# Start of a Strassen w_out stage: two operand sums formed earlier, operands halved ahead of weight tiles, two weight loads issued sooner

## The chip, the cores and the metric

The kernel runs on one core of one Trainium2 chip. TensorE (PE) multiplies, with its weight loads shown apart as PEld; VectorE (DVE), ScalarE (ACT) and GpSimd (POOL) work on tiles; SyncE (SP) issues all DMAs here. The metric is the device time of one execution in microseconds, lower is better.

## The reference

A block with attention in a sliding window, and a gated MLP beside it, over 2048 tokens of width 576, all in float32. What the change touches is the last product of the MLP and the end of the block.

```python
z1 = z[..., :Fh]                       # Fh = 2304
z2 = _layernorm(z[..., Fh:], axis=-1)
g = jnp.einsum("ts,bsf->btf", w_sp, z2) + b_sp[None, :, None]
return jnp.einsum("bsf,fd->bsd", z1 * g, w_out)     # the w_out stage
...
s = _A_ref(xn, A_wqkv, A_wo)
g = _silu(_B_ref(xn, B_w_in, B_w_sp, B_b_sp, B_w_out))
return x + s * g
```

## The kernel before, in words

Every float32 product is made as three matmuls in a reduced format: each operand is halved into an upper half (`act.activation` with a copy on ACT, line 115) and a lower half (source minus upper half on DVE, line 116). PE multiplies upper by upper, upper by lower and lower by upper. `split` (lines 114 to 116) is this pair, so every halved tile costs one ACT and one DVE instruction, in this order, and the third matmul of each block needs DVE's.

The stage before (`acc`, line 1429) is the token mixing with `w_sp`; its gated result y is stored to DRAM (`y_d<-z1t`, line 1365). The w_out stage then multiplies y (2304 by 2048) with w_out (2304 by 576), in 2 by 2 blocks. Tokens come in eight pairs p of two groups of 128 rows. Pair 0 is computed directly: four operands (a12, a11, a21, a22), each with two products of 27 matmuls, 54 per step. Pairs 1 to 7 use the Strassen-Winograd scheme: seven products P1 to P7 of 27 matmuls, whose left operands are blocks of y or sums of them, and whose right operands are blocks of w_out or the sums T1 to T4 prepared earlier in DRAM (`t_d`).

The list `SEQ` (line 1303) fixes the order of the steps: pair 0's four, then of pair 1 P4, P1, P6, P2, P5, P7, then of pair 2 P4, P1, then P3 of pair 1, P6 of pair 2, and so on. Step i is matmuled, and then the operand of step i+3 is formed by `formed(i + 3)`, which calls `y_form`. Operands live in three tiles o0, o1, o2 in turn, so o(i mod 3) is free when step i has been multiplied. The engines are not reordered by a scheduler here: each runs its instructions in the order in which the code is written, and so does SP with its DMAs.

Blocks of y for a pair are loaded (`y_load`, line 1317) into fixed places: a11 and a21 into the tile `zr`, a22 and a12 into the tile `u2` (named `u2_15512` in the orders, `u` in the trace); from pair 2 on one of a12 and a22 goes to a `wr` buffer instead. When `y_form` makes P1's operand, three sums follow on DVE, in place (lines 1327 to 1329): a22 becomes a21 + a22, a21 becomes a11 - a21, a11 becomes the new a22 - a11. The new a11 is P6's operand, the new a21 is P7's, the new a22 is P5's.

Weights come in 13 parts of up to five blocks of 128 rows: parts 7 to 12 are fetched by `w_fetch` (line 1272) into one of two `wr` buffers and halved by `w_halve` into b5 and w0 to w4. Parts 9 to 12 (w1 to w4) hold T2 and T1, which P6 and P5 use. The sum T3, for P7, goes in three pieces (`t3_fetch`, line 1288; `t3_halve`) over the place of B12, through the same two `wr` buffers: a fetch waits until the part that was in its buffer has been halved. w2, w3 and w4 lie in the pool `yp`, which takes over the memory of the pool `wk`, where the tiles `z1t` were; so w2 is written only when the last stores `y_d<-z1t` have read them.

Rows are finished by `finish` (lines 1498 to 1506): DVE multiplies the attention output `sv` by the gate `gs` (line 1501) and adds `xr`, the input (line 1502), SP stores the row (line 1503), and `load_end` loads `sv` and `xr` of the next row (lines 1491, 1492).

Of the kernel before, what the change touches and what calls it, by code (L numbers as in the profile page):

```python
# [12 lines left out]
ALU = mybir.AluOpType  # L13
# [51 lines left out]
def kernel(  # L65
# [14 lines left out]
    act, dve, pool, pe, sp = nc.scalar, nc.vector, nc.gpsimd, nc.tensor, nc.sync  # L80
# [155 lines left out]
    with ExitStack() as early:  # L236
# [281 lines left out]
        with ExitStack() as ph:  # L518
# [259 lines left out]
            def finish(u, ou):  # L778

                g, half = UNITS[u]  # L780
                cs = slice(half * HS, half * HS + HS)
                den = aa.tile([P, HS // 32], F32, name="den")
                rp = ap_.tile([P, HS], F32, name="rp", bufs=1) if u < NU - 1 else f32(slots[4][:, 0:HS])
                def invert():
                    dve.reciprocal(den, den)
                    t = use("dve", 270) - clock + 300
                    after(t + (1500 if u < NU - 2 else 300), lambda: sp.dma_start(r_d[u].rearrange("h (a b) -> (h a) b", b=HS // 32), den))
                    for i in range(4):
                        after(t + (FETCH_AT if u < NU - 2 else 4500) + 400 * i, partial(sums, i))

                def sums(i):
                    sp.dma_start(rp[32 * i:32 * i + 32, :], r_d[u][i:i + 1, :].to_broadcast([32, HS]))

                def divide(a, n=4):
                    hs = slice(a * HS // n, (a + 1) * HS // n)
                    pool.tensor_tensor(ou[:, hs], ou[:, hs], rp[:, hs], ALU.mult)
                    use("pool", 2900 / n)

                def store(i):
                    h = 4 * g + i  # L800
                    sp.dma_start(o_d[h * DH:(h + 1) * DH, cs], ou[32 * i:32 * i + DH, :])

                if u == NU - 1:
                    def put_last():
                        dve.reciprocal(den, den)
                        sp.dma_start(r_d[u].rearrange("h (a b) -> (h a) b", b=HS // 32), den)

                    last.extend([lambda: sp.dma_start(den, ou[DH::32, :]), put_last,
                                 lambda: [sums(i) for i in range(4)], lambda: [divide(a, 2) for a in range(2)],
                                 lambda: [store(i) for i in range(4)]])  # L810
                else:
                    after(busy["act"] - clock + 1000, lambda: sp.dma_start(den, ou[DH::32, :]))
                    sooner = 10000 if u == NU - 2 else 0
                    after(max(INVERT_AT - sooner, 4500), invert)
                    parts[u] = [partial(divide, a) for a in range(4)] + [partial(store, i) for i in range(4)]
                    for ns in DIVIDE_AT:
                        after(ns - sooner + (3500 if sooner else 0), partial(part, u))
# [388 lines left out]
    with ExitStack() as ph:  # L1206
# [58 lines left out]
        def w_fetch(i, home):  # L1265
            n = 3 if i == 12 else 5
            w_raws[i] = w_raw(home, i, n)
            done = 0
            while done < n:
                o, k0 = divmod(5 * i + done, 9)  # L1270
                m = min(n - done, 9 - k0)
                sp.dma_start(w_raws[i][:, done:done + m], w_rows(W_ORDER[o], k0, m))
                done += m

        def w_halve(i, home, name):
            raw = w_raws.pop(i)
            n = raw.shape[1]
            t = home.tile([P, 8 * ZW if home in (xp, zc) else n * D], F32R, name=name)[:, :n * D]
            t = t.rearrange("p (a k c) -> p a k c", a=2, c=288)
            split(t[:, 0], t[:, 1], raw)  # L1280
            w_tiles.append(t)
# [16 lines left out]
        quads, operands, homes = {}, {}, {}  # L1298
# [10 lines left out]
        def y_load(p, name):  # L1309
            i, j = int(name[1]) - 1, int(name[2]) - 1  # L1310
            t = p + 4 * (p // 4) + 4 * i
            if p > 1 and name == ("a12", "a22")[p % 2]:
                q = homes["o2"].tile([P, 1440], F32, name="wr", bufs=2)[:, :9 * P]
            else:
                q = QUAD_AT[name]
            quads[p, name] = q = q.rearrange("p (f t) -> p f t", t=P)
            sp.dma_start(q, y_d[j * FB:(j + 1) * FB, t * P:(t + 1) * P].rearrange("(f p) t -> p f t", p=P))

        def y_form(i):
            p, prod = SEQ[i]  # L1320
            home = yw if i % 3 < 2 else homes["o2"]
            o = home.tile([P, 2304], F32R, name=f"o{i % 3}", bufs=1).rearrange("p (a f t) -> p a f t", a=2, t=P)
            q = {name: quads.get((p, name)) for name in QUAD_AT}
            split(o[:, 0], o[:, 1], q[OF.get(prod, prod)])
            operands[p, prod] = o
            if prod == "P1":
                dve.tensor_tensor(q["a22"], q["a21"], q["a22"], ALU.add)
                dve.tensor_tensor(q["a21"], q["a11"], q["a21"], ALU.subtract)
                dve.tensor_tensor(q["a11"], q["a22"], q["a11"], ALU.subtract)
            if prod == "P2":  # L1330
                dve.tensor_tensor(q["a12"], q["a12"], q["a11"], ALU.subtract)
# [80 lines left out]
        def run_lazy(n):  # L1412
            for _ in range(n):
                if lazy:
                    lazy.pop(0)()
# [71 lines left out]
        def load_end():  # L1487
            if row_order:
                r = end_rows(*row_order.pop(0))
                t = [yp.tile([P, D], F32, name=n, bufs=1 + (n == "xr")) for n in ("sv", "xr", "gs")]  # L1490
                sp.dma_start(t[0], s_d[r, :])
                sp.dma_start(t[1], x[r, :])
                ends.append((r, *t))
# [4 lines left out]
        def finish(c0=0, c1=D):  # L1498
            r, sv, xr, gs = ends[0]
            cs = slice(c0, c1)  # L1500
            dve.tensor_tensor(sv[:, cs], sv[:, cs], gs[:, cs], ALU.mult)
            dve.tensor_tensor(xr[:, cs], xr[:, cs], sv[:, cs], ALU.add)
            sp.dma_start(out[r, cs], xr[:, cs])
            if c1 == D:
                ends.pop(0)
                load_end()

        def small_tile(p, name):
            small[p, name] = t = (right if name in ("t1", "t4") else yp).tile([P, 288], F32, name=name, bufs=1)
# [53 lines left out]
        for i, (p, prod) in enumerate(SEQ):  # L1563
            if p == 0:
                first_pair(i, prod)
                if i == 0:
                    y_load(1, "a11")
                    y_load(1, "a21")
                    w_halve(8, right, "w0")
                    w_fetch(9, right)  # L1570
                formed(i + 3)
                if i == 0:
                    run_lazy(6)
                    w_halve(9, right, "w1")
                    w_fetch(10, right)
                    run_lazy(len(lazy))
                    gates.close()
                    yp = open_pool(ph, "yp")
                    load_end()
                    y_load(1, "a12")  # L1580
                if i in (1, 3):
                    silu_of(0, banks[f"C{i // 2 + 1}1"][:, :288])
                    silu_of(1, banks[f"C{i // 2 + 1}2"][:, :288])
                if i == 1:
                    w_fetch(11, right)
                    w_halve(10, yp, "w2")
                    finish()
                if i == 2:
                    w_fetch(12, right)
                    w_halve(11, yp, "w3")  # L1590
                    t3_fetch(right, T3_PARTS[0])
                if i == 3:
                    finish()
                    w_halve(12, yp, "w4")
                    t3_fetch(right, T3_PARTS[1])
                continue
            o = operands.pop((p, prod))
            c = product(o, (p, BANK_OF[prod]), W_OF[prod])
            sums = sum_up(p, prod, c)
            if i == 5:  # L1600
                t3_halve(T3_PARTS[0])
                t3_fetch(right, T3_PARTS[2])
            if i in (6, 7):
                t3_halve(T3_PARTS[i - 5])
            formed(i + 3)
            for half in sums:
                silu_of(*half)
            if prod in ("P7", "P3"):
                if (p, prod) == (LAST, "P3"):
                    finish(288, D)  # L1610
                else:
                    finish()
            if (p, prod) == (LAST, "P2"):
                finish(0, 288)
# [71 lines left out]
```

## Time and profile before

| what | us |
|---|---|
| median of three runs | 1860.63 (1852.94 to 1866.33) |
| the profiled execution | 1859.84 |
| its span, first to last instruction | 1857.8 |
| what lies around the span | 2.0 |
| first matmul of the w_out stage (c, line 1520) | 1641.82 |
| start of the last run of matmuls without a wait | 1705.79 |

Times inside the trace count from the start of the span. A row of a timeline gives start, duration, engine, line, operation and tiles, and in brackets how long the engine sat idle before it and what ended that. Starts of consecutive matmuls lie closer together than their durations, since they are pipelined. SPq rows are the issue of a DMA, not its transfer.

### The profile page before, as it was taken

What the parts mean: (1) busy time and instruction counts of PE and PEld (TensorE: products, weight loads), DVE (VectorE), ACT (ScalarE), POOL (GpSimd) and SP (SyncE); (2) the same over time, 40 slices, a digit from 0 to 9 for tenths busy, and PEclk for the clock granted to TensorE, in tenths of its full rate; (3) what the DMA queues carried; (4) which work ended last, traced back from release to release, by engine and by line L of the source; (5) the groups of instructions that cost most, each with busy time, mean ns of one, the idle gap of its engine ahead of it and who ended that gap; (6) DMA issues with size and microseconds to landing.
All of it is one profiled execution on the core that took longest, in us unless ns stands there. A gap on an engine that the chain in (4) does not pass through costs nothing.

```text
span 1857.8 us, 38152 instructions
## 1 busy us (share of the span) xinstructions
PE 1819.5 (98%) x14357; PEld 1584.6 (85%) x14357; DVE 1138.2 (61%) x2283; ACT 946.8 (51%) x1756; POOL 433.3 (23%) x507
## 2 busy tenths in 40 slices
PE   8999999999999999999999999999999999998998
PEld 8999999997777777776988878888888888898998
DVE  6321333457766777761246788667876567758876
ACT  5433222315666576677467566465554544444443
POOL 3332333434465455555000000121200000000000
PEclk9999999999999999999999999999999999999999
DMA  8895688887576666655876777789776556796554
GB/s 272 190 234 161 232 283 281 297 251 218 155 190 168 189 180 184 182 156 145 254 247 227 238 238 245 257 290 304 252 260 234 186 182 199 251 264 186 161 159 133
DMA packets 266920, 405.75 MB, mean 218 GB/s; under 512 B 52336, under 2 KB 180592, under 8 KB 266608
## 3 DMA queue, kind: packets, MB, share of 16 engines
q1 hardware_dynamic: 266736, 403.32, 70.3%
q8 instruction: 113, 1.85, 0.4%
q14 instruction: 71, 0.58, 0.1%
HBM read 285.35 MB, written 117.09 MB: 217 GB/s over the span
## 4 chain that ended last, share of the span: by engine, by line
PE 81%; DMA 6%; DVE 6%; ACT 3%; SPq 2%; issue 2%; POOL 0%; ACTq 0%; DVEq 0%; POOLq 0%
PE acc L1429 35%; PE mb L206 9%; PE c L1520 7%; PE ma L206 7%; PE ma L669 6%; PE mb L669 5%; PE ops L750 4%; PE tps L722 2%; PE sp L598 2%; PE wops L1155 1%; SPq L363 1%; DMA st_d<-qkhl 1%; DMA z_d<-z1o 1%; DVE junk L602 1%; PE ma L380 1%
## 5 line engine op out<-in xcount | busy, mean ns | idle before, releaser
L1429 PE MATMUL acc<-sph,zh 128*128 128x512 f32 x1008 | 392.3, 389 | 1.7 <-ACT so L1188 1.7
L1429 PE MATMUL acc<-spl,zh 128*128 128x512 f32 x1008 | 392.7, 390 | 1.2 <-DVE spl L116 1.0
L1429 PE MATMUL acc<-sph,zl 128*128 128x512 f32 x1008 | 392.2, 389 | 0.0
L602 DVE CUSTOM_DVE_ANT_0 junk<-sp,band 128x384 bf16<-128x384 f32 (+1 forms) x512 | 276.3, 540 | 113.4 <-PE sp L598 32.6
L726 ACT ACTIVATE pt<-tps 128x384 f32<-128x384 f32 (+2 forms) x576 | 231.3, 441 | 119.4 <-PE tps L722 75.8
L116 DVE TENSOR_TENSOR spl<-spr,sph 128x1024 fp32r<-128x1024 f32 x168 | 209.9, 1249 | 41.9 <-ACT sph L115 40.9
L669 PE MATMUL mb<-b,z1wh 64*128 64x512 f32 x648 | 224.5, 399 | 2.1 <-ACT z1o L674 1.7
L1429 PEld LDWEIGHTS acc<-spl,zh 128*128 128x128 f32 x1008 | 189.2, 188 | 42.4 <-DVE spl L116 3.2
L669 PE MATMUL ma<-b,z1wh 64*128 64x512 f32 x648 | 223.9, 398 | 0.7 <-ACT zt L946 0.4
L1429 PEld LDWEIGHTS acc<-sph,zh 128*128 128x128 f32 x1008 | 189.2, 188 | 41.1 <-ACT so L1188 2.2
L1429 PEld LDWEIGHTS acc<-sph,zl 128*128 128x128 f32 x1008 | 189.2, 188 | 39.4
L115 ACT ACTIVATE zh<-b 128x384 fp32r<-128x384 f32 x168 | 87.4, 520 | 209.2 <-PE acc L1429 209.1
L115 ACT ACTIVATE sph<-spr 128x1024 fp32r<-128x1024 f32 x168 | 176.0, 1047 | 16.2 <-DMA spr<-in_w_sp_dram 8.5
L722 PE MATMUL tps<-att 56*128 56x384 f32 (+1 forms) x576 | 176.7, 345 | 3.2 <-DMA att<-mhl 1.6
L116 DVE TENSOR_TENSOR zl<-b,zh 128x384 fp32r<-128x384 f32 x168 | 99.6, 593 | 122.7 <-ACT zh L115 122.6
L598 PE MATMUL sp<-att 54*128 54x384 f32 (+1 forms) x512 | 160.7, 348 | 1.6 <-DVE mx L602 1.5
L1520 PE MATMUL c<-b,o 128*128 128x288 f32 x1056 | 143.8, 295 | 2.7 <-DVE o L116 1.8
L1520 PEld LDWEIGHTS c<-b,o 128*128 128x128 f32 x1056 | 140.9, 188 | 3.6 <-DVE o L116 2.3
L947 DVE BATCH_NORM_STATS2 st<-zt 128x6 f32<-128x384 f32 x96 | 49.3, 548 | 132.0 <-ACT zt L946 131.7
L669 PE MATMUL ma<-b,z1wl 64*128 64x512 f32 x324 | 128.0, 395 | 0.0
L669 PE MATMUL mb<-b,z1wl 64*128 64x512 f32 x324 | 127.7, 394 | 0.0
L722 PEld LDWEIGHTS tps<-att 56*128 56x128 f32 x576 | 99.4, 184 | 31.6 <-issue 9.5
(220 smaller groups left out, 4181.4 us busy)
## 6 DMA issues: line engine op xcount, KB each, us to landing
spr<-sc_d SPq DMA_DIRECT2D x96, 512.0 KB
spr<-in_w_sp_dram SPq DMA_DIRECT2D x72, 512.0 KB
zr<-z_d SPq DMA_DIRECT2D x144, 192.0 KB
z_d<-zt SPq DMA_DIRECT2D x48, 384.0 KB
z_d<-z1o SPq DMA_DIRECT2D x72, 256.0 KB
z1t<-z_d SPq DMA_DIRECT2D x72, 256.0 KB
y_d<-z1t SPq DMA_DIRECT2D x72, 256.0 KB
a<-in_w_sp_dram SPq DMA_DIRECT2D x64, 256.0 KB
```

What stands on the lines that cost most here:

```text
L115: act.activation(hi, src, AF.Copy)
L116: dve.tensor_tensor(lo, src, f32(hi), ALU.subtract)
L206: pe.matmul(banks[h][:, :n], *both[h][i], start=i == 0, stop=i == STEPS - 1)
L598: pe.matmul(ps[:, :w], q_of(u, j)[0:54, i * P:(i + 1) * P], k_of(u, j)[0:54, k0:k0 + w], start=True, stop=True)
L602: dve.tensor_tensor_reduce(out=junk[:, :w], in0=ps[:, :w], in1=band[:, m0:m0 + w], scale=1.0, scalar=-3.0e38, op0=ALU.add, op1=ALU.max, ac ...
L669: pe.matmul(ps, w, x_, start=n == 0, stop=n == STEPS - 1)
L722: pe.matmul(ps[:, :m * P], k_of(u, j)[:, (kb - base) * P:(kb - base + 1) * P], q_of(u, j)[:, (a - lo) * P:(a - lo + m) * P], start=True, s ...
L726: act.activation(pt[:, j, d0:d0 + n * P], ps[:, (qa - a) * P:(qa - a + n) * P], AF.Exp, scale=scale)
L750: pe.matmul(o_ps[c][32 * j:32 * j + 32, (qa - 4 * c) * P:(hi - 4 * c + 1) * P], vgs[u][:, kb - k0, j * VW:j * VW + 32], pt[:, j, (qa - kb) ...
L947: dve.bn_stats(st2[:, s, pc, :], zv)
L1429: pe.matmul(acc[j], z[:, ps], w[:, cs], start=s == i == 0 and n in OPENS, stop=s == 7 and i == 2, skip_group_check=True)
L1520: pe.matmul(banks[key][:, :288], y, w, start=begin and k == n == 0, stop=close and k == 8 and n == 2, skip_group_check=True)
```

## The change

In the code of the first four steps (i = 0 to 3), nothing of the arithmetic changes:

- Part 11 of the weights (for w3) is fetched right behind part 10, at i = 0, ahead of the last two stores of y; before, at i = 1. Part 12 (for w4) is fetched ahead of the first `finish`, not behind it.
- For pair 1, the first two of the three sums are taken at i = 1, right after P4's operand is halved, and not at i = 2 after P1's. The third stays.
- The operands of P1 and P6 are halved ahead of w2 and w3. Before, w2 and w3 stood ahead of them, one step earlier in the code.
- w4, and the second piece of T3, come ahead of the second `finish`.
- In every `finish`, the loads for the next row are issued ahead of the store of this row.

```diff
+        def y_sums(p):
+            a11, a21, a22 = (quads[p, name] for name in ("a11", "a21", "a22"))
+            dve.tensor_tensor(a22, a21, a22, ALU.add)
+            dve.tensor_tensor(a21, a11, a21, ALU.subtract)
...
             if prod == "P1":
-                dve.tensor_tensor(q["a22"], q["a21"], q["a22"], ALU.add)
-                dve.tensor_tensor(q["a21"], q["a11"], q["a21"], ALU.subtract)
+                if p > 1:
+                    y_sums(p)
                 dve.tensor_tensor(q["a11"], q["a22"], q["a11"], ALU.subtract)
...
             dve.tensor_tensor(xr[:, cs], xr[:, cs], sv[:, cs], ALU.add)
-            sp.dma_start(out[r, cs], xr[:, cs])
             if c1 == D:
                 ends.pop(0)
                 load_end()
+            sp.dma_start(out[r, cs], xr[:, cs])
...
                     w_fetch(10, right)
+                    w_fetch(11, right)
                     run_lazy(len(lazy))
...
+                if i == 1:
+                    y_sums(1)
+                if i == 3:
+                    w_halve(11, yp, "w3")
+                    t3_fetch(right, T3_PARTS[0])
                 if i in (1, 3):
                     silu_of(0, banks[f"C{i // 2 + 1}1"][:, :288])
                     silu_of(1, banks[f"C{i // 2 + 1}2"][:, :288])
-                if i == 1:
-                    w_fetch(11, right)
+                if i == 2:
                     w_halve(10, yp, "w2")
+                    w_fetch(12, right)
                     finish()
-                if i == 2:
-                    w_fetch(12, right)
-                    w_halve(11, yp, "w3")
-                    t3_fetch(right, T3_PARTS[0])
                 if i == 3:
-                    finish()
                     w_halve(12, yp, "w4")
                     t3_fetch(right, T3_PARTS[1])
+                    finish()
                 continue
```

PE's order is the same in both programs. On DVE, in the stretch from the lower half of P4's operand (o1) to that of P2's (the second o1), before:

```order
L116 TENSOR_TENSOR o1_21546<-u2_15512,o1_21546 128x1152
L116 TENSOR_TENSOR w2_21553<-wr_21477,w2_21553 128x1440
L1501 TENSOR_TENSOR sv_21486<-sv_21486,gs_21488 128x576
L1502 TENSOR_TENSOR xr_21487<-xr_21487,sv_21486 128x576
L116 TENSOR_TENSOR o2_21620<-zr_15511,o2_21620 128x1152
L1327 TENSOR_TENSOR u2_15512<-zr_15511,u2_15512 128x1152
L1328 TENSOR_TENSOR zr_15511<-zr_15511 128x1152
L1329 TENSOR_TENSOR zr_15511<-u2_15512,zr_15511 128x1152
L116 TENSOR_TENSOR w3_21628<-wr_21551,w3_21628 128x1440
L116 TENSOR_TENSOR o0_21687<-zr_15511,o0_21687 128x1152
```

and after, from the same instruction on (o2 is P1's operand, o0 is P6's):

```order
L116 TENSOR_TENSOR o1_21548<-u2_15512,o1_21548 128x1152
L1321 TENSOR_TENSOR u2_15512<-zr_15511,u2_15512 128x1152
L1322 TENSOR_TENSOR zr_15511<-zr_15511 128x1152
L116 TENSOR_TENSOR o2_21611<-zr_15511,o2_21611 128x1152
L1334 TENSOR_TENSOR zr_15511<-u2_15512,zr_15511 128x1152
L116 TENSOR_TENSOR w2_21615<-wr_21477,w2_21615 128x1440
L1506 TENSOR_TENSOR sv_21488<-sv_21488,gs_21490 128x576
L1507 TENSOR_TENSOR xr_21489<-xr_21489,sv_21488 128x576
L116 TENSOR_TENSOR o0_21682<-zr_15511,o0_21682 128x1152
L116 TENSOR_TENSOR w3_21685<-wr_21480,w3_21685 128x1440
L116 TENSOR_TENSOR w4_21692<-wr_21618,w4_21692 128x864
L1506 TENSOR_TENSOR sv_21622<-sv_21622,gs_21624 128x576
```

All three sums and P1's lower half have moved from behind w2 and the first row to ahead of them, P6's operand stands ahead of w3, and w4 ahead of the second row.

On SP, from the fetch of part 10 (`wr_21477`, two DMAs) on, before (`wr_21551` is part 11, `wr_21626` part 12, `wr_21631` and `wr_21703` the first two pieces of T3):

```order
L1272 DMA wr_21477<-t_d_69 128x4x288
L1272 DMA wr_21477<-t_d_69 128x288
L1365 DMA y_d_62<-z1t_21256 128x512
L1365 DMA y_d_62<-z1t_21258 128x512
L1491 DMA sv_21486<-s_d_68 128x576
L1492 DMA xr_21487<-in_x_dram 128x576
L1317 DMA u2_15512<-y_d_62 128x9x128
L1272 DMA wr_21551<-t_d_69 128x5x288
L1503 DMA out_0_dram<-xr_21487 128x576
L1491 DMA sv_21559<-s_d_68 128x576
L1492 DMA xr_21560<-in_x_dram 128x576
L1272 DMA wr_21626<-t_d_69 128x3x288
```

and after, from the second DMA of part 10 on (`wr_21480` is part 11, `wr_21618` part 12, `wr_21688` and `wr_21695` the pieces of T3):

```order
L1272 DMA wr_21480<-t_d_69 128x5x288
L1370 DMA y_d_62<-z1t_21256 128x512
L1370 DMA y_d_62<-z1t_21258 128x512
L1496 DMA sv_21488<-s_d_68 128x576
L1497 DMA xr_21489<-in_x_dram 128x576
L1317 DMA u2_15512<-y_d_62 128x9x128
L1272 DMA wr_21618<-t_d_69 128x3x288
L1496 DMA sv_21622<-s_d_68 128x576
L1497 DMA xr_21623<-in_x_dram 128x576
L1511 DMA out_0_dram<-xr_21489 128x576
L1288 DMA wr_21688<-t_d_69 128x3x288
L1288 DMA wr_21695<-t_d_69 128x5x288
```

Part 11 has moved ahead of the last two stores of y and the first row's loads, part 12 and the second piece of T3 ahead of a row each, and each row's store behind the next row's loads.

## The prediction

> **What bounds the kernel now.** I read the busy times by stage first, then PE's timeline across the stage that the change edits, then who fed each gap (DVE, ACT, SP), and last the chain of waits. Three stretches of the w_out stage, and a part of the first, with busy time and count of each engine, granted clock, DMA share and GB/s:
>
> ```profile
> 1641.82:1677.60 35.78, 35.78 (x271) 35.64 (x269) 24.07 (x25) 13.50 (x12) 0.00 (x0) 1.00 0.88 263
> 1677.60:1705.79 28.19, 23.04 (x166) 21.87 (x165) 23.23 (x24) 14.24 (x19) 0.00 (x0) 1.00 0.59 170
> 1705.79:1851.80 146.01, 146.01 (x1105) 146.01 (x1105) 112.03 (x117) 58.35 (x76) 0.00 (x0) 1.00 0.54 160
> 1656.00:1674.70 18.70, 18.70 (x144) 18.70 (x143) 8.45 (x8) 5.63 (x6) 0.00 (x0) 1.00 0.91 275
> ```
>
> In the last long stretch PE never stops: 1105 matmuls in 146.01 us, 132.1 ns each. The first stretch also runs at that pace (271 in 35.78). The middle one doesn't: 166 matmuls are worth 21.9 us and take 28.19. So about 6.3 us is all that PE loses in this stage, 0.3% of the kernel; the change cannot win more than that and what the tail gives. The waits themselves are these, PE's:
>
> ```profile
> 1679.09 0.54 PE L1520 MATMUL c<-w,o 128*128 128x288 f32 x2 [1.40 <-ACT o L115]
> 1680.65 3.57 PE L1520 MATMUL c<-w,o 128*128 128x288 f32 x25 [1.02 <-DVE o L116]
> ...
> 1692.48 0.54 PE L1520 MATMUL c<-b,o 128*128 128x288 f32 x2 [0.93 <-ACT o L115]
> 1694.39 5.16 PE L1520 MATMUL c<-b,o 128*128 128x288 f32 x37 [1.38 <-DVE o L116]
> ...
> 1705.79 3.58 PE L1520 MATMUL c<-b,o 128*128 128x288 f32 x25 [0.42 <-DVE o L116]
> ```
>
> Always two matmuls run, then the third waits for the lower half: the operand is late, not the weights. The steps are P6 of pair 1 (1679.09), P7 of pair 1 (1692.48) and P3 of pair 1 (1705.79). The gaps add up to 5.15 us; the missing 1.1 of the 6.3 is the modelled end of the last matmul before each gap. Now DVE:
>
> ```profile
> 1661.08 1.36 DVE L116 TENSOR_TENSOR o<-u,o 128x1152 fp32r<-128x1152 f32 x1 [3.33 <-ACT o L115]
> 1669.32 1.66 DVE L116 TENSOR_TENSOR w<-wr,w 128x1440 fp32r<-128x1440 f32 x1 [6.88 <-ACT w L115]
> 1670.89 0.75 DVE L1501 TENSOR_TENSOR sv<-sv,gs 128x576 f32<-128x576 f32 x1
> ...
> 1672.36 1.35 DVE L116 TENSOR_TENSOR o<-zr,o 128x1152 fp32r<-128x1152 f32 x1
> 1673.63 1.35 DVE L1327 TENSOR_TENSOR u<-zr,u 128x1152 f32<-128x1152 f32 x1
> ...
> 1676.40 1.36 DVE L1329 TENSOR_TENSOR zr<-u,zr 128x1152 f32<-128x1152 f32 x1
> ...
> 1681.98 1.05 DVE L116 TENSOR_TENSOR w<-wr,w 128x864 fp32r<-128x864 f32 x1
> 1682.95 1.35 DVE L116 TENSOR_TENSOR o<-u,o 128x1152 fp32r<-128x1152 f32 x1
> ...
> 1695.43 1.36 DVE L116 TENSOR_TENSOR o<-u,o 128x1152 fp32r<-128x1152 f32 x1 [0.72 <-ACT o L115]
> ...
> 1698.97 1.36 DVE L1327 TENSOR_TENSOR u<-zr,u 128x1152 f32<-128x1152 f32 x1 [0.91 <-DMA zr<-y_d]
> ...
> 1704.38 1.35 DVE L116 TENSOR_TENSOR o<-u,o 128x1152 fp32r<-128x1152 f32 x1
> ```
>
> DVE idles 6.88 us ahead of w2 and then does everything that P6 needs in one go, ending with the third sum at 1677.76. ACT shows what each was waiting for:
>
> ```profile
> 1667.88 1.41 ACT L115 ACTIVATE w<-wr 128x1440 fp32r<-128x1440 f32 x1 [4.80 <-DMA y_d<-z1t]
> 1674.80 1.41 ACT L115 ACTIVATE w<-wr 128x1440 fp32r<-128x1440 f32 x1 [4.46 <-DMA wr<-t_d]
> 1677.88 1.16 ACT L115 ACTIVATE o<-zr 128x1152 fp32r<-128x1152 f32 x1 [1.67 <-DVE zr L1329]
> ...
> 1679.53 0.92 ACT L115 ACTIVATE w<-wr 128x864 fp32r<-128x864 f32 x1
> ...
> 1682.77 0.93 ACT L115 ACTIVATE b<-wr 128x864 fp32r<-128x864 f32 x1 [0.66 <-DMA wr<-t_d]
> ...
> 1689.97 1.41 ACT L115 ACTIVATE b<-wr 128x1440 fp32r<-128x1440 f32 x1 [5.22 <-DMA wr<-t_d]
> 1694.23 1.17 ACT L115 ACTIVATE o<-u 128x1152 fp32r<-128x1152 f32 x1 [1.36 <-DMA u<-y_d]
> ```
>
> The first is w2, held by the last store of y; 1689.97 is T3's second piece, which stands ahead of P7's operand on ACT; 1694.23 is pair 2's a22, for its P4. SP's issues behind these, and the chain's three pieces that matter:
>
> ```profile
> 1659.87 0.96 SPq L1365 DMA_DIRECT2D y_d<-z1t  x2
> 1661.77 0.32 SPq L1491 DMA_DIRECT2D sv<-s_d  x1
> ...
> 1664.12 1.22 SPq L1272 DMA_DIRECT2D wr<-t_d  x1
> ...
> 1674.58 0.38 SPq L1272 DMA_DIRECT2D wr<-t_d  x1
> 1679.36 0.37 SPq L1288 DMA_DIRECT2D wr<-t_d  x1
> ...
> 1683.50 0.38 SPq L1288 DMA_DIRECT2D wr<-t_d  x1
> ...
> 1687.95 0.36 SPq L1317 DMA_DIRECT2D u<-y_d  x1
> ```
>
> ```profile
> 1660.37 7.41 DMA y_d<-z1t
> ...
> 1848.50 0.34 SPq L1503
> 1848.84 0.05 issue
> 1848.89 0.42 SPq L1491
> ...
> 1849.36 3.40 DMA xr<-in_x_dram
> ...
> 1852.85 0.46 DVE xr L1502
> ```
>
> **The change, part by part.**
>
> *Sums and P1's operand ahead of w2.* Four instructions (three sums, P1's lower half) of 1.27 to 1.39 us, 5.3 us in all, go into the 6.88 us of idle, from 1662.4 to 1667.8. They cost nothing there: that cover ends only when w2 comes, and w2 comes later than before (next item). This removes P6's wait at its source.
>
> *Part 11 ahead of the stores.* The fetch, 720 KB, is now issued at about 1659.9 instead of 1664.12. The last two stores line up behind it, and w2 still waits for them. In this stretch DMA is 91% busy and moves 275 GB/s, so 737,280 bytes are worth 2.7 us: the stores land at 1670.5 where ACT saw them at 1667.88. From below: nothing, if the fetch fills gaps of the 9% idle time. From above: the stores' second issue slips from 1660.37 to SP's next free moment, about 1661.8, and takes its 7.41 us plus 2.7, so 1671.9. I take 1670.5, since the queue is nearly full. A page's price stands apart: the Trainium skill, "DMA: Bandwidth & Descriptors", section "Anatomy of one DMA — SWDGE (gpsimd) path", has bytes over 436 GB/s for the moving part, which would be 1.7 us; by it the stores land at 1669.6 and the total would be 0.9 us lower. The 275 GB/s measured here decides.
>
> *The DVE run behind w2.* Its starts follow from the rows' spacing: DVE's w2 1.44 us after ACT's, at 1671.9; then 1.57 for w2, 1.47 for the row, 1.27 for P6's lower half, 1.57 for w3, 0.97 for w4, again 1.47 for the second row. So P6's lower half is done at 1676.3 (PE reaches P6 at 1677.6: its wait is gone), w4 at 1678.9, and P2's lower half runs from 1680.3 to 1681.6, where PE wants it at about 1681.4. Part 12 is fetched behind w2 at 1673.5, and ACT must have it by 1676.9 for this. T3's first piece, as large, took 3.4 us (1679.36 to 1682.77), which just does; part 12 itself took at most 4.95 before, behind a row's loads (1674.58 to 1679.53, where ACT didn't wait for it), and that would cost 1.5. I take the 3.4: the row's loads now come behind it.
>
> *T3's second piece.* It needs w4 halved: issued at 1678.9 instead of 1683.50. P7's operand on ACT, behind it, comes 4.6 us sooner, and PE wants P7 at 1677.6 + 3 x 27 x 0.1321 = 1688.3 instead of about 1691.5. Its wait goes, or shrinks to tenths.
>
> *What is late next: pair 2's a22.* SP issues its load after P5's lower half, 5.0 us after P2's lower half starts (1682.95 to 1687.95). With P2's at 1680.3 that is 1685.3, 2.7 us sooner; taking the same 6.28 us until ACT can read it (1687.95 to 1694.23) it is there at 1691.6. PE is at pair 2's P4 at 1691.9, and needs ACT's and then DVE's half: this is a new wait of about 2 us. Behind it DVE runs without a pause to P3's lower half: 1695.43 to 1705.73 before, 10.30 us, of which 0.91 was the wait for a21, whose load also moves up and lands in time. So P3's lower half ends at 1691.6 + 1.2 + 9.39 = 1702.2, where it was 1705.73. From there on PE ran without a wait and does so again. **Gain 3.5 us.**
>
> *Loads ahead of each row's store.* Every store goes out some 0.9 us later, every load 0.39 us sooner (0.34 and 0.05). Inside the stage it costs nothing: no matmul waits in 146 us, and a row's buffer is wanted again only two rows later. At the end it counts: the last row's add at 1852.85 is held by a load on the chain, and the last lower row waits behind it on DVE. Bounds 0 and 0.39 + the same again if both loads wait; **0.4 us.**
>
> The sum: 1859.84 - 3.5 - 0.4 = 1855.9, call it 1856.0. The profiled execution lies 0.8 under the median of 1860.63, and the three runs spread from 1852.94 to 1866.33, so the measurement moves more than the change does. About 1% is what a measurement of this kernel can tell from no change.
>
> **The rivals.**
>
> *All of PE's waits go.* If a22 of pair 2 lands when PE gets there, the whole 6.3 and 0.4 are won: 1853.1. For it speaks that DMA in the middle stretch is 59% busy, so loads could land faster than 6.28 us; against it, that the a22 load is not moved in the code, and now queues behind the same bytes.
>
> *The wait only moves.* If a22 lands no sooner than before (1694.23), because T3's piece and a row's loads now crowd just ahead of it, DVE's run from 1695.43 loses only the 0.91 for a21: 1859.84 - 0.9 - 0.4 = 1858.5. The 0.59 DMA share speaks against it.
>
> *Slower: the stores fall too far back.* w2, then P6, w3 and w4 stand in one line on ACT and on DVE, all behind these stores. P2's lower half starts 9.8 us after they land; before, it started at 1682.95, so it is later than before once they land after 1673.2, and from there each us later costs one. At 1676 it would be 2.8 - 0.4: 1862.2. My upper bound of 1671.9 stops short of it. The Trainium skill, on the same page, section "Queues, rings and completion order", says that on each engine descriptors are consumed in ring order, which is the mechanism, and the rule that speaks against this change; the trace agrees in that part 11, issued at 1664.12 behind the others, was there only at 1674.80, 10.7 us later.
>
> **How the numbers follow.** The forecast has 0.52, all waits gone 0.17, the wait only moves 0.21, slower 0.10. None of them, priced out, lies over 1% (18.6 us) from the time before, so within 1% has 0.97, and the rest is for the spread of the runs: 0.02 faster, 0.01 slower. The range goes from 1850, all waits gone and a run some 3 us low, to 1863, the slow rival with a run 1 us high; the runs' own spread makes most of it.
>
> **What would show it.** Right: no wait of PE at P6 (near 1677.6); w2 on ACT at 1670 to 1671.5, still released by `y_d<-z1t`; T3's second piece issued near 1679; the 1105-matmul run beginning near 1702; a wait of some 2 us at pair 2's P4, with a22's load behind it; the last add near 1852.85 - 3.9. Wrong: a wait at P1 or P2 of pair 1, w2 after 1673, or a22 no sooner than 1694. Then the gain is below 1.5 us, and the error is in how the queue shares the bytes. If the last run begins at 1699.5, I had a22 too late.

## The result, and the profile after

| what | before | after |
|---|---|---|
| median, us (lowest to highest, 22 runs each) | 1861.11 (1852.94 to 1867.46) | 1857.09 (1850.40 to 1863.25) |
| ratio of the times, 95% interval | | 0.9981 [0.9972, 0.9990] |
| last matmul's start to the end of the span, us | 6.0 | 5.7 |

The change saves 0.19%, 3.5 us by the ratio, between 1.9 and 5.2 by its interval. The forecast was 1856.0, 3.8 us under its own profiled execution.

Executions differ by more than this before the w_out stage begins (last section), so all places below count from the first matmul of the stage: 1641.82 in the trace of before, 1642.98 in that of after. A number like 28.15 is such a distance. First the stage in three stretches, split at P6 of pair 1 and at the last run of matmuls without a wait, as before: length, then busy time and count of PE, PEld, DVE, ACT and POOL, granted clock, DMA share and GB/s.

```profile
1642.98:1678.70 35.72, 35.72 (x272) 35.72 (x270) 27.32 (x28) 16.66 (x18) 0.00 (x0) 1.00 0.87 248
1678.70:1702.77 24.07, 22.55 (x167) 21.73 (x165) 20.06 (x21) 11.13 (x14) 0.00 (x0) 1.00 0.70 221
1702.77:1848.80 146.03, 146.03 (x1105) 146.02 (x1105) 112.39 (x118) 58.43 (x76) 0.00 (x0) 1.00 0.54 160
```

Only the middle stretch has changed: it takes 24.07 us where it took 28.19. Six steps of 27 matmuls and the first two of P3 begin in it, 164 in both kernels, worth 21.7 us at 132.1 ns, so PE loses 2.4 us there and lost 6.5 before. (The rows count 167 and 166, since they include matmuls that began earlier; by these counts the losses are 2.0 and 6.3, and that is how the prediction and the expectations give them.) The granted clock is 1.00 throughout, in both kernels. What is left of the waits stands in PE's timeline:

```profile
1678.70 3.73 PE L1525 MATMUL c<-w,o 128*128 128x288 f32 x27
1682.26 4.12 PE L1525 MATMUL c<-b,o 128*128 128x288 f32 x27
...
1694.83 1.59 PE L1525 MATMUL c<-b,o 128*128 128x288 f32 x10 [0.86 <-DVE o L116]
...
1702.77 3.58 PE L1525 MATMUL c<-b,o 128*128 128x288 f32 x25 [0.54 <-DVE o L116]
```

P6 (1678.70) runs its 27 matmuls in one piece, P7's wait is gone as well, and there are two waits: a new one at pair 2's P4 (1694.83), and P3's old one (1702.77). From P6's first start to P2's at 1682.26 there are 3.56 us, 27 x 0.132. By the starts of neighbouring matmuls less 0.132 the two waits are 1.02 and 0.70 us, since a matmul's modelled end hides 0.16 us of each: a matmul is shown 0.29 us long, and the next starts 0.13 us after it. All waits below are counted by starts. DVE, with the two sums at lines 1321 and 1322 and the third at 1334:

```profile
1662.24 1.36 DVE L116 TENSOR_TENSOR o<-u,o 128x1152 fp32r<-128x1152 f32 x1 [3.33 <-ACT o L115]
1663.64 1.36 DVE L1321 TENSOR_TENSOR u<-zr,u 128x1152 f32<-128x1152 f32 x1
1665.03 1.36 DVE L1322 TENSOR_TENSOR zr<-zr 128x1152 f32<-128x1152 f32 x1
1666.31 1.35 DVE L116 TENSOR_TENSOR o<-zr,o 128x1152 fp32r<-128x1152 f32 x1
1667.69 1.36 DVE L1334 TENSOR_TENSOR zr<-u,zr 128x1152 f32<-128x1152 f32 x1
1672.58 1.66 DVE L116 TENSOR_TENSOR w<-wr,w 128x1440 fp32r<-128x1440 f32 x1 [3.53 <-DMA xr<-in_x_dram]
...
1675.62 1.35 DVE L116 TENSOR_TENSOR o<-zr,o 128x1152 fp32r<-128x1152 f32 x1
1676.89 2.62 DVE L116 TENSOR_TENSOR w<-wr,w 128x1440 fp32r<-128x1440 f32 x2
...
1693.42 1.36 DVE L116 TENSOR_TENSOR o<-u,o 128x1152 fp32r<-128x1152 f32 x1 [2.14 <-ACT o L115]
```

All three sums and P1's lower half now stand in the old idle stretch, one behind the other from 1663.64 to 1669.05, and 3.53 us of idle time are still left before w2. P6's lower half (1675.62) is done at 1676.97, 1.7 us before PE begins P6. ACT and SP over the same time:

```profile
1671.13 1.42 ACT L115 ACTIVATE w<-wr 128x1440 fp32r<-128x1440 f32 x1 [5.26 <-DMA xr<-in_x_dram]
...
1673.50 1.40 ACT L115 ACTIVATE w<-wr 128x1440 fp32r<-128x1440 f32 x1
...
1677.33 0.93 ACT L115 ACTIVATE w<-wr 128x864 fp32r<-128x864 f32 x1 [1.62 <-DMA wr<-t_d]
...
1684.79 1.42 ACT L115 ACTIVATE b<-wr 128x1440 fp32r<-128x1440 f32 x1
...
1692.22 1.17 ACT L115 ACTIVATE o<-u 128x1152 fp32r<-128x1152 f32 x1 [1.43 <-DMA u<-y_d]
```

```profile
1659.23 2.31 SPq L1272 DMA_DIRECT2D wr<-t_d  x3
1661.58 2.11 SPq L1370 DMA_DIRECT2D y_d<-z1t  x2
...
1674.27 0.37 SPq L1272 DMA_DIRECT2D wr<-t_d  x1
...
1678.56 1.34 SPq L1288 DMA_DIRECT2D wr<-t_d  x2
...
1686.41 0.37 SPq L1317 DMA_DIRECT2D u<-y_d  x1
```

In SP's rows part 11 is the third fetch of the first group, ahead of the last two stores. w2 comes on ACT at 1671.13, 28.15 after the stage's start, where before it came at 26.06. Its bracket names a load of xr: that is what ended last by the profile, not what w2 needs, and the last store landed at the same time, 1671.06. w3 follows at 1673.50 without a wait, since part 11 had landed at 1669.52.

How w2 came to be 2.1 us later can be seen on SP. Its DMAs use eight completion semaphores in turn, so one is issued only when the one eight places ahead of it has landed. With part 11 ahead of the stores, the last of the six stores waits for the first of them to land; in the second profile of the changed kernel (changed_again, below) the chain of waits shows this, from the first store's issue by way of the last store's to w2 on ACT:

```profile
1652.54 6.41 DMA y_d<-z1t
...
1658.96 8.17 DMA y_d<-z1t
...
1667.21 1.42 ACT w L115
```

In all eight profiles with the early fetch the last store is issued 19.8 to 20.4 us after the stage's start, and w2 is on ACT 7.8 to 8.8 us behind it; in the six without, it is issued at 18.5 to 18.8, and w2 follows 7.4 to 8.1 us behind it. So the shift shows as a later issue, by some 1.4 us on average, and a longer way from there, by some 0.7.

T3's second piece is the later issue of the group at 1678.56, done by 1679.90, and is halved at 1684.79 (41.81) where it was at 1689.97 (48.15). The tail, by the chain of waits:

```profile
1844.67 0.77 DVE xr L1507
...
1845.46 0.32 SPq L1496
...
1845.88 3.51 DMA xr<-in_x_dram
...
1849.51 0.46 DVE xr L1507
```

From one add to the next are 4.84 us, where there were 5.14 (1847.71 to 1852.85). The load starts 0.44 us sooner behind the add and takes 0.11 us longer.

### The profile page after: what moved, and what is told of

It is laid out like the page before. It is cut to its first block, busy times and chain, and to the rows that moved or that the text cites. A ratio compares the mean times of both kernels' runs of the same rounds, so it can differ in the third digit from the quotient of the medians.

```text
span 1854.5 us, 38148 instructions
## 1 busy us (share of the span) xinstructions
PE 1821.4 (98%) x14357; PEld 1588.3 (86%) x14357; DVE 1138.4 (61%) x2283; ACT 948.4 (51%) x1756; POOL 432.0 (23%) x507
## 4 chain that ended last, share of the span: by engine, by line
PE 84%; DVE 6%; DMA 5%; SPq 2%; ACT 2%; issue 2%; POOL 0%; DVEq 0%; ACTq 0%; POOLq 0%
PE acc L1434 35%; PE mb L206 12%; PE c L1525 8%; PE ma L669 6%; PE mb L669 5%; PE ops L750 4%; PE ma L206 4%; PE tps L722 3%; PE sp L598 2%; PE wops L1155 2%; SPq L363 1%; DMA xr<-in_x_dram 1%; PE ma L380 1%; DMA st_d<-qkhl 1%; DVE junk L602 1%
## 5 line engine op out<-in xcount | busy, mean ns | idle before, releaser
L947 DVE BATCH_NORM_STATS2 st<-zt 128x6 f32<-128x384 f32 x96 | 49.2, 547 | 131.4 <-ACT zt L946 131.3
```

The lines of the kernel that those rows point to most:

```text
L947: dve.bn_stats(st2[:, s, pc, :], zv)
```

## The experiments

The table counts PE's loss over the whole stage: the last matmul's start less the first's, less 1538 x 0.1321 = 203.2 us, for the 1539 matmuls of line 1520 (1525 after). The starts stand in the view of that line; it has the shortest, median and longest duration, then first and last start, here for before, after and the experiment that matters most:

```profile
L1520 PE MATMUL c<-b,o x1056: 288/294/402, 1641.8 to 1851.8; 128*128 128x288 f32 x176
```

```profile
L1525 PE MATMUL c<-b,o x1056: 288/294/406, 1643.0 to 1848.7; 128*128 128x288 f32 x176
```

```profile
L1525 PE MATMUL c<-b,o x1056: 288/294/398, 1640.5 to 1844.9; 128*128 128x288 f32 x176
```

These are 210.0, 205.7 and 204.4, so losses of 6.8, 2.5 and 1.2 us (the table uses starts to the hundredth). The middle stretch alone, by the counts of its rows, has 0.5 to 0.6 us less than the whole stage. A loss that an expectation gives may be of either kind, so what counts is the difference from the changed kernel.

| kernel | ratio to before [95%] | PE's loss, us | w2 on ACT | waits of PE, us |
|---|---|---|---|---|
| before | | 6.8 | 26.06 | P6 2.75, P7 2.63, P3 0.58 |
| before_again | one execution | 6.7 | 26.00 | P6 2.69, P7 1.54, P3 0.51 |
| the changed kernel | 0.9981 [0.9972, 0.9990] | 2.6 | 28.15 | P2 0.28, pair 2's P4 1.02, P3 0.70 |
| changed_again | one execution | 2.9 | 28.28 | P2 0.28, P4 1.21, P3 0.69 |
| late_fetch | 0.9971 [0.9960, 0.9982] | 1.2 | 26.25 | P4 0.23, P3 0.71 |
| late_fetch_again | one execution | 0.9 | 26.27 | P3 0.69 |
| sums_back | 0.9984 [0.9973, 0.9994] | 3.0 | 28.43 | P2 0.76, P4 0.97, P3 0.71 |
| tiles_first | 0.9993 [0.9982, 1.0004] | 4.8 | 28.14 | P1 1.60, P6 0.56, P4 1.03, P3 0.68 |
| sums_alone | 0.9989 [0.9976, 1.0002] | 4.6 | 26.25 | P6 0.38, P2 0.73, P7 2.14, P3 0.62 |
| store_first | 0.9976 [0.9965, 0.9988] | 3.7 | 28.55 | P2 0.77, P7 0.69, P4 1.02, P3 0.70 |
| row_before_w4 | 0.9996 [0.9984, 1.0008] | 5.0 | 28.49 | P2 1.56, P7 2.43, P3 0.52 |
| p5_first | 0.9980 [0.9967, 0.9992] | 3.4 | 28.76 | P5 0.87, P7 0.93, P3 0.83 |
| p5_first_p3_first | 0.9969 [0.9958, 0.9980] | 1.6 | 28.42 | P5 0.24, P7 0.92 |
| late_fetch_p3_first | 0.9967 [0.9950, 0.9984] | 1.7 | 26.86 | P7 0.15, P4 1.02 |

P4 is pair 2's throughout, all other steps pair 1's. The waits add up to 0.2 to 0.9 us less than the loss, in part because the matmul that follows the one that waited starts 0.24 us after it and not 0.13. In before_again 1.4 us more are lost without a wait: right behind P6's wait, from 1681.94 to 1685.05, the granted clock is 0.50, and 13 matmuls take 0.24 us each. P7's wait is 1.1 us shorter there, since PE comes later. Two profiles of one kernel differ by 0.1 to 0.3 us in the loss, so differences under half a microsecond are not read.

### Part 11 fetched behind the stores again: late_fetch

The changed kernel with the fetch of part 11 back where it was before, one step later.

```diff
                     w_fetch(10, right)
-                    w_fetch(11, right)
                     run_lazy(len(lazy))
...
+                if i == 1:
+                    w_fetch(11, right)
                 if i == 2:
                     w_halve(10, yp, "w2")
```

> The changed kernel, with part 11 fetched at its old place, behind the last two stores of y and the first row's loads. Times from the stage's first matmul. My theory: the stores land sooner, so w2 starts on ACT at 26.1 us, not 28.15; but w3 then waits for its own part until 33, and w4 with T3's second piece comes 0.5 to 1 later than in the changed kernel (37.2 against 36.6). PE loses 2 to 3 us behind P6, against 2.0 in the changed kernel and 6.3 before: the early fetch is worth under 1 us. Rival, the sooner loads are what wins: P7's wait is back and PE loses over 4.

Measured: 1853.94 us against 1860.28. The loss does not stay or grow: it falls to 1.2 us. On ACT:

```profile
1666.74 1.41 ACT L115 ACTIVATE w<-wr 128x1440 fp32r<-128x1440 f32 x1 [3.37 <-DMA sv<-s_d]
...
1671.71 1.41 ACT L115 ACTIVATE w<-wr 128x1440 fp32r<-128x1440 f32 x1 [1.21 <-DMA wr<-t_d]
...
1673.60 0.93 ACT L115 ACTIVATE w<-wr 128x864 fp32r<-128x864 f32 x1
...
1678.54 0.93 ACT L115 ACTIVATE b<-wr 128x864 fp32r<-128x864 f32 x1 [1.72 <-DMA wr<-t_d]
...
1681.92 1.41 ACT L115 ACTIVATE b<-wr 128x1440 fp32r<-128x1440 f32 x1 [1.39 <-DMA wr<-t_d]
```

The stage begins at 1640.50 here, so w2 is at 26.24 (28.15 in the changed kernel), w3 at 31.21 (30.52), w4 at 33.10 (34.35), T3's second piece at 41.42 (41.81). w3 waits 1.21 us for its part and is 0.7 later; w4 and all that follows are sooner all the same. The first finished row and P6's half stand behind w2 and ahead of w3; DVE then waits only 0.57 us for w3. Part 12, for w4, is fetched when w2 is halved, at 29.39 and not at 31.28, so w4's part arrives in time. a22 of pair 2, the cause of the new wait, is on ACT at 1688.35, 47.85 against 49.24. The early fetch thus brings one tile 0.7 us sooner and delays the line of work behind w2 by 1.9.

The Trainium skill, "DMA: Bandwidth & Descriptors", section "Rules for kernel authors", advises to issue a DMA early and to wait for it late. Taken alone, it speaks for the early fetch. The runs here don't bear it out where a store that others wait for stands behind the fetch: PE's loss is 1.2 us with the late fetch and 2.6 with the early one.

### The same, and before and the changed kernel, once more: late_fetch_again, changed_again, before_again

No edit. They tell how far one profile of a kernel lies from another.

> late_fetch once more. My theory: w2 starts on ACT by 26.8 us after the stage's first matmul and the loss over the stage stays under 2.0. If the first profile was chance, the loss is 2.4 or more.

> The changed kernel once more, to see how far a profile repeats. My theory says that w2 follows the landing of the stores, so w2's start may move by some tenths and the loss by as much: loss over the stage 2.2 to 3.4 us against 2.57, waits at the same three places. If the loss of late_fetch (1.23) was chance, it can come out here as well.

> The kernel before once more: the same three waits, loss over the stage 6.2 to 7.4 us (6.78), w2 on ACT at 26 to 27 us after the stage's first matmul.

Measured: losses of 0.9, 2.9 and 6.7 us, so the gap between late and early fetch is 1.3 in the first pair of profiles and 2.0 in the second. The second profile of before shows why the first estimate of a late fetch was too dear. There w3 began on ACT at 1674.80, 32.98 after the stage's start; here, with the stage beginning at 1643.17:

```profile
1674.44 1.41 ACT L115 ACTIVATE w<-wr 128x1440 fp32r<-128x1440 f32 x1 [2.81 <-DMA wr<-t_d]
```

That is 31.27, and both profiles of late_fetch have it at 31.2 to 31.4. The one profile of before on which the prediction rests had this fetch 1.7 us late; w2 was in the same place in both (26.06 and 26.00). before_again's loss agrees with before's in its sum only: 1.4 us of it are the lower clock named under the table.

### Two sums back behind P1's half: sums_back

```diff
             if prod == "P1":
-                if p > 1:
-                    y_sums(p)
+                y_sums(p)
...
-                if i == 1:
-                    y_sums(1)
```

> The changed kernel, with the two sums again behind the lower half of P1's operand, but all of it still ahead of w2. My theory: nothing changes, since DVE idles 3.5 us ahead of w2 and the sums fit there as well: PE's loss stays at 2.0, within 0.2, and no wait at P6. Rival, the place of the sums is what wins: P6 waits again by 2 us or more, and the total is 2 us over the changed kernel's.

Measured: 1857.4 us against 1860.28, loss 3.0. P6 has no wait; the largest change is at P2, 0.76 instead of 0.28:

```profile
1683.35 3.57 PE L1524 MATMUL c<-b,o 128*128 128x288 f32 x25 [0.60 <-DVE o L116]
...
1695.28 1.58 PE L1524 MATMUL c<-b,o 128*128 128x288 f32 x10 [0.81 <-DVE o L116]
```

Once the operands stand ahead of the tiles, the sums fit into DVE's idle stretch from either place: four instructions, 5.4 us, in about 8.9. The loss is 0.1 to 0.4 us over the changed kernel's two, where the expectation allowed 0.2; that is hardly more than two profiles of one kernel differ by. w2 came 0.1 to 0.3 us later in this profile as well (28.43).

### Only the sums moved: sums_alone

The kernel before, with nothing changed but the place of the two sums.

```diff
             if prod == "P1":
+                if p > 1:
+                    y_sums(p)
-                dve.tensor_tensor(q["a22"], q["a21"], q["a22"], ALU.add)
-                dve.tensor_tensor(q["a21"], q["a11"], q["a21"], ALU.subtract)
...
+                if i == 1:
+                    y_sums(1)
```

> The kernel before, with nothing but the two sums moved to behind P4's operand. My theory: P6's operand still waits on ACT behind w3, whose part lands at 33.0 us after the stage's first matmul, so its lower half comes 1.4 us sooner than before, not 4.3, and everything behind it shifts by the same: PE's loss 6.3 - 1.4 = 4.9. Rival, the sums alone do it: loss 2 to 3 us, as in the changed kernel.

Measured: 1858.42 us against 1860.28, ratio not clear of 1; the loss falls by 2.2 us to 4.6. P6's wait shrinks from 2.75 to 0.38, but P7's hardly (rows: P2, P7's two):

```profile
1686.02 3.56 PE L1525 MATMUL c<-b,o 128*128 128x288 f32 x25 [0.56 <-DVE o L116]
...
1693.68 0.53 PE L1525 MATMUL c<-b,o 128*128 128x288 f32 x2 [0.46 <-ACT o L115]
1695.58 5.16 PE L1525 MATMUL c<-b,o 128*128 128x288 f32 x37 [1.37 <-DVE o L116]
```

The gain is larger than expected: w3 was on ACT at 31.48 here, not at the 33.0 taken from the one profile of before, so P6's lower half came 2.5 us sooner, not 1.4. P7 is a separate matter: it waits for T3's second piece. The sums are worth 2.2 us alone and nothing clear of the scatter beside the other moves. They and the operands' new place are two ways to the same gain, so the parts don't add up.

### w2 and w3 ahead of the operands again: tiles_first

```diff
-                if i == 3:
-                    w_halve(11, yp, "w3")
-                    t3_fetch(right, T3_PARTS[0])
...
-                if i == 2:
+                if i == 1:
                     w_halve(10, yp, "w2")
                     w_fetch(12, right)
                     finish()
+                if i == 2:
+                    w_halve(11, yp, "w3")
+                    t3_fetch(right, T3_PARTS[0])
```

> The changed kernel, with w2 and w3 again ahead of P1's and P6's operands; sums, loads and row order as changed. My theory: w2, held by the stores until 28.1 us after the stage's first matmul, now holds P1's operand too: a wait of about 1.5 us at P1, a shorter one at P6, T3's second piece issued near 39 (36.6 in the changed kernel, 41.7 before), and PE's loss from P1 on 4 to 5 us. Rival, operand order doesn't matter once the sums are early: the loss stays near 2.0.

Measured: 1858.85 us against 1860.28, loss 4.8: 2.0 to 2.3 us more than the changed kernel. PE waits where the changed kernel does not, at P1 and P6:

```profile
1674.14 3.58 PE L1525 MATMUL c<-b,o 128*128 128x288 f32 x25 [1.44 <-DVE o L116]
1678.37 3.57 PE L1525 MATMUL c<-w,o 128*128 128x288 f32 x25 [0.40 <-DVE o L116]
```

With w2 (28.14) in front, P1's own operand waits for the stores of y, and only the first two sums are left in DVE's idle stretch. P1's wait is new: before, w2 came 2.1 us sooner.

### The second row finished ahead of w4 and T3's second piece: row_before_w4

```diff
                 if i == 3:
+                    finish()
                     w_halve(12, yp, "w4")
                     t3_fetch(right, T3_PARTS[1])
-                    finish()
```

> The changed kernel, with the second row finished ahead of w4 and T3's second piece, as before the change. My theory: DVE stands in the row until its sv has landed, so w4's lower half comes 2 to 3 us later, T3's second piece is issued near 39.4 us after the stage's first matmul (36.6 in the changed kernel, 41.7 before), P2 and P7 of pair 1 wait, and PE's loss is 3.5 to 5 us. Rival, T3's piece has slack: the loss stays at 2.0, since a22 of pair 2 is what is late.

Measured: 1859.98 us against 1861.20, loss 5.0, 2.2 to 2.5 us over the changed kernel; nearly all of the gain is gone. T3's second piece goes out at 40.20, not 36.55, and P2 and P7 wait:

```profile
1690.11 3.58 PE L1525 MATMUL c<-b,o 128*128 128x288 f32 x25 [1.40 <-DVE o L116]
...
1698.02 0.53 PE L1525 MATMUL c<-b,o 128*128 128x288 f32 x2 [0.72 <-ACT o L115]
1699.93 5.16 PE L1525 MATMUL c<-b,o 128*128 128x288 f32 x37 [1.39 <-DVE o L116]
```

A finished row is two DVE instructions of 0.76 us that nothing on PE needs. But it waits for loads, and w4's lower half, queued behind it, holds T3's fetch. Of the parts of the change that were undone one at a time, this one costs most, about as much as the operands' place (2.0 to 2.3 us).

### Store ahead of the loads again: store_first

```diff
+            sp.dma_start(out[r, cs], xr[:, cs])
             if c1 == D:
                 ends.pop(0)
                 load_end()
-            sp.dma_start(out[r, cs], xr[:, cs])
```

> The changed kernel, with each row's store again ahead of the next row's loads. My theory: only the tail shows it: from the start of the next to last full-row add to the last lower-row add held by a load 5.1 us (as before) against 4.8, so 0.3 to 0.4 us in the total; PE's loss behind P6 stays at 2.0 within 0.3. Rival, the stores in front also hold the loads of the first rows and with them w4 and T3: the loss is over 2.5.

Measured: 1856.67 us against 1861.20, loss 3.7, tail 5.96 us against 5.73. The tail bears out the forecast's last term, at 0.1 to 0.3 us: with the loads first it is 5.7 to 5.9 us in all profiles, with the store first 6.0. The loss was to stay, and is 0.9 to 1.2 higher, with waits at P2 and P7:

```profile
1684.59 3.57 PE L1525 MATMUL c<-b,o 128*128 128x288 f32 x25 [0.61 <-DVE o L116]
1692.57 3.87 PE L1525 MATMUL c<-b,o 128*128 128x288 f32 x27 [0.53 <-DVE o L116]
```

P2's wait is no mark of the store's place: sums_back, which has the loads first, waits as long there (0.76). P7 waits for T3's second piece, which was issued at 36.95 and halved at 43.87, 6.9 us later, where it took 5.3 and 5.8 in the changed kernel's two profiles. Whether the store's bytes stand in its way or this landing merely was a late one, a single profile can't say; the times don't show a loss (ratio 0.9976, its interval overlaps the changed kernel's). This stays open.

### P5 ahead of P2, and P3's half ahead of pair 2's sums: p5_first, p5_first_p3_first, late_fetch_p3_first

p5_first changes two entries of the order list:

```diff
-               (1, "P4"), (1, "P1"), (1, "P6"), (1, "P2"), (1, "P5"), (1, "P7")]
+               (1, "P4"), (1, "P1"), (1, "P6"), (1, "P5"), (1, "P2"), (1, "P7")]
```

p5_first_p3_first has this too, and makes pair 2's three sums behind P3's lower half; late_fetch_p3_first has only this second edit, with the late fetch:

```diff
             if prod == "P1":
-                if p > 1:
+                if p > 2:
                     y_sums(p)
-                dve.tensor_tensor(q["a11"], q["a22"], q["a11"], ALU.subtract)
+                if p != 2:
+                    dve.tensor_tensor(q["a11"], q["a22"], q["a11"], ALU.subtract)
+            if (p, prod) == (1, "P3"):
+                y_sums(2)
+                dve.tensor_tensor(quads[2, "a11"], quads[2, "a22"], quads[2, "a11"], ALU.subtract)
```

> The changed kernel, with P5 of pair 1 taken ahead of P2, so that pair 2's a22 can be loaded one step sooner. My theory of what is left (a22's load, then DVE's long run): the wait at pair 2's P4 (0.9 us in the timeline) goes, but the sums still wait for a21, so P3's lower half is hardly sooner: P3's wait grows to over 1 us and the total loss stays between 1.4 and 2.0. Rival, a22 alone is the limit: the loss falls under 0.8.

> The same, and pair 2's three sums behind the lower half of P3's operand instead of ahead of it. My theory: both waits go: P3's lower half is done by 56 us after the stage's first matmul, where PE wants it at 57.4, and P6 of pair 2 has its own in time or 0.4 late; the loss is under 0.6 and the total 1.4 to 2.0 us under the changed kernel's. Rival, DVE is full there and the wait only moves on to P6 of pair 2: the loss stays at 1.5 or more.

> The changed kernel with part 11 fetched at its old place, and pair 2's three sums behind the lower half of P3's operand. If w2's wait for the stores and DVE's run ahead of P3 are all that is left, both waits that late_fetch still had (0.2 at pair 2's P4, 0.7 at P3) shrink to the first alone: PE's loss over the whole stage is 0.8 to 1.0 us (2.6 in the changed kernel, 1.2 in late_fetch), and the total 1.5 to 2 us under the changed kernel's. If DVE is full there, P6 of pair 2 waits instead and the loss stays at 1.2.

Measured: 1858.1, 1856.59 (both against 1861.20) and 1853.27 us (against 1859.53). p5_first takes pair 2's P4 wait away, but P5, now in P2's place, waits 0.87 and P7 0.93, so the loss does not fall (3.4, where 1.4 to 2.0 was expected). With P3's half first, P3's wait is gone in both kernels that have the edit, and the loss of the early-fetch kernel falls to 1.6, again more than was expected (under 0.6), because P7's wait stays:

```profile
1692.44 5.15 PE L1529 MATMUL c<-b,o 128*128 128x288 f32 x37 [0.77 <-DVE o L116]
```

late_fetch_p3_first has a wait at pair 2's P4 once more:

```profile
1695.89 1.58 PE L1529 MATMUL c<-b,o 128*128 128x288 f32 x10 [0.87 <-DVE o L116]
```

Its w2 came at 26.86, 0.6 later than in late_fetch, so late landings and the edit are mixed in its 1.7, where 0.8 to 1.0 was expected. By the ratios the three best (0.9967 to 0.9971) cannot be told apart, nor are they clear of the changed kernel, whose interval overlaps theirs. By the profile alone late_fetch is the best, at 0.9 and 1.2 us.

## Why the prediction was right, point by point

Forecast and measurement from the stage's first matmul, in us:

| step of the prediction | forecast | measured (after, changed_again) |
|---|---|---|
| w2 on ACT, behind the stores | 28.7 | 28.15, 28.28 |
| P6's wait | gone | gone, gone |
| P2's lower half late by | 0.2 | 0.28, 0.28 |
| T3's second piece issued | 37.1 | 36.55, 36.67 |
| P7's wait | gone | gone, gone |
| a22 of pair 2 on ACT | 49.8 | 49.24, 49.50 |
| new wait at pair 2's P4 | 2 | 1.02, 1.21 |
| last run of matmuls begins | 60.4 | 59.79, 60.06 |
| gain in the tail | 0.4 | 0.3, 0.3 |

**The sums and operands.** P6's wait went as forecast, and for the reason given: the three sums and P1's lower half fit into DVE's idle stretch ahead of w2. sums_back has the same four there in another order, and P6 does not wait; tiles_first has only two of them there, and P1 and P6 wait. What carries the gain beside the other moves is thus the operands' place ahead of the tiles; the two sums may stand on either side of P1's half once this is so.

**The early fetch.** The size was near: 2.7 us forecast for 720 KB, 2.1 and 2.3 measured as w2's shift from 26.06 and 26.00. The Trainium skill's 436 GB/s ("DMA: Bandwidth & Descriptors", section "Anatomy of one DMA — SWDGE (gpsimd) path", which is about DMAs that GpSimd issues) would make it 1.7, as an estimate; the measured shift lies between the two. The prediction took it as the time of part 11's bytes, and there the nearness is in part luck: some 1.4 us of it show as a later issue of the last store, behind an earlier store's landing, which the prediction had only in its upper bound and without this wait. No run separates part 11's bytes from its place among SP's DMAs, so this cause stays open. The prediction does carry the shift on into its sum, through P2's half, a22's load and P3's half, but it never asks what the change would win with the fetch left behind the stores, and puts the wait at pair 2's P4 down as something that is late next. late_fetch shows that this wait is mostly the fetch's own: with the stores first, it is 0.23 in one profile and absent in the other. The change would have won 1.3 to 2.0 us more of PE's time without this part.

**T3's second piece.** Issued 0.5 sooner than forecast, as w2 was. row_before_w4 shows that its place ahead of the row is worth 2.2 to 2.5 us.

**The new wait.** The place and what PE waits for were right, the size was not: 2 us forecast, 1.02 measured (1.21 in the second profile). a22's load was issued at 43.43 (forecast 43.5), and was on ACT 5.8 us later, not 6.28 as in the trace of before. So DVE's half ended at 51.8, not 52.4; and PE itself came there about 0.5 later than reckoned, after its 0.28 at P2 and other small delays. Both take from the wait. Since PE's lateness is lost time as well, only the 0.5 to 0.6 of the sooner load shows in the sum: the last run begins at 59.79 and not at 60.4.

**The sum.** 3.5 for the stage and 0.4 for the tail were forecast. The stage gained 4.2 (6.8 to 2.6) in the first pair of profiles and 3.8 (6.7 to 2.9) in the second, the tail 0.3. The 6.3 us that the prediction gave as all that PE loses counted two matmuls too many; it is 6.5 in that stretch and 6.8 in the stage. The times say 3.5 [1.9, 5.2]; the medians differ by 4.0.

**The rivals.** "The wait only moves" needed a22 no sooner than 52.4: it came at 49.2. "Slower" needed the stores after 31.4: they came at 28.1. Its mechanism is real, though, and takes back a quarter to a third of what the rest of the change wins: 1.3 to 2.0 of 5.5 to 5.8. "All of PE's waits go" did not happen here; late_fetch comes nearest to it, with 0.9 to 1.2 us left, of which P3 has 0.7.

What stays open: how part 11's fetch delays the last store, store_first's wait at P7, and whether the best of the variants is faster than the changed kernel in time. The three best were not timed against it directly.

## What to carry to other kernels

In a line of work that two engines share, put what TensorE needs next ahead of what merely has arrived, and look at whole lines: a sum, an operand and a weight tile in the wrong order cost the same wait, so undoing one move alone may show nothing. Before a fetch is issued earlier, look at what stands behind it in the same queue: if another engine waits for a store there, the fetch can hold up that store's issue and its landing (w2 came 2.1 to 2.3 us later here), and a tile that cannot be used sooner gains nothing in return. When a trace has the price of a landing, take it from two executions if there are two; one had it 1.7 us off.

## What the runs showed of the hardware that was not expected

Most of the scatter in time arises before this stage, where no edit acts. The stage's first matmul starts at 1637.1 in p5_first and at 1649.0 in row_before_w4, with these spans and clocks:

```profile
core 0: 1849.5 us, clock 0.999
```

```profile
core 0: 1862.9 us, clock 0.994
```

Most of the 11.9 us go with the granted clock. In row_before_w4 it is 0.50 for 20.4 us ahead of the stage, in stretches of 3.4 and 6.8 us, which is 10.2 us of PE's time at full clock if PE is busy then, as an estimate; in p5_first it is never lowered there. In the w_out stage itself the clock is 1.00 in all profiles but before_again, where one such stretch of 3.4 us falls right behind P6's wait, and the loss repeats within 0.3 us. A stage's own length resolves changes of 1 us that the time of the whole kernel, at five rounds, leaves within its interval.

Landings of the same fetch differ between executions of the same program: ACT began to halve part 11 at 32.98 and at 31.27 after the stage's start in the two profiles of before.
